# Moving the gather of one channel to steps 12 to 24, loading x first, and sharing weight conversion between engines

## The chip, the cores and the metric

One core of one Trainium2 chip. The metric is device microseconds of one execution of the whole program. A ratio is the mean time of one kernel's fast runs over that of the other's of the same rounds, so it is not quite the ratio of the medians quoted beside it.

## The reference, cut to what matters

```python
# x: (8, 3008, 256) float32; w_in: (256, 2048), w_out: (2048, 256)
X = np.fft.fft(np.fft.fft(x, axis=1), axis=2).real.astype(np.float32)
h = X.reshape(8 * 3008, 256) @ w_in
g = np.where(h > 0, h, np.exp(np.minimum(h, 0)) - 1)     # elu
return (g @ w_out).astype(np.float32)
```

The two weights reach the kernel as 64-bit floats (a float32 array times a NumPy scalar). The kernel converts them to 32 bits itself, with integer and float operations on their words.

## The kernel before

The sequence transform is done with matmuls on folded rows of x (sums and differences of rows s and 3008-s, and of the two halves). The channel transform is folded into w_in ("folding": `fold_block`, four blocks of 512 columns). The main loop has 376 steps. A step takes 256 columns of the transformed data through two of the 16 blocks of d_ff: first matmuls P and Q into a bank H, the elu on VectorE and ScalarE, sums on GpSimd, second matmuls into banks pA to pD. Everything is emitted in an order given by times in `at(t, ...)`, and each engine keeps that order. T is one step.

Channel 128 of the channel transform needs a row of its own: `r128`, spread over all partitions (`Rb`), times the last row of the folded weights, turned into a column (`wex`). Its input is one channel of x for all batches, gathered element by element:

```python
def load_ext(j, s0, s1):                      # 16 calls, 17 DMAs
    def copy(s0, s1, row, step):
        nc.sync.dma_start(out=t[:, s0:s1],
            in_=bass.AP(tensor=xt, offset=x.offset + row * ND + 128,
                        ap=[[SEQ * ND, NB], [step * ND, s1 - s0], [1, 1]]))
    ...
def fold_block(q):                            # w_in's block q times the channel transform
    for part, dst in ((128, Ws), (0, Wc)):
        ps = bank("H")                        # three H banks in all
        for h in range(2):
            mm(ps, CC[:, h*256+part : h*256+part+128], w1[q][:, h], h == 0, h == 1)
        act(dst[:, cols], ps)                 # ScalarE evicts
def spread_last_row(q):
    nc.sync.dma_start(out=wx_dr[:, c], in_=Ws[127:128, c])
    nc.sync.dma_start(out=wex[:, 4*q : 4*q+4], in_=wx_dr[:, c].rearrange(...))
def even_part(i):                             # E of step i waits for wex of its block
    ... scalar_tensor_tensor(out=S.E[:, c], in0=Rb[:, cols(i)],
            scalar=wex[:, f:f+1], in1=S.H[:, c], op0=mult, op1=add)
# schedule
for n in range(16): at((0.5 + 0.55 * n) * T, ... load_ext ...)
at(9.2 * T, get_ext); at(11 * T + 1.35, fold_ext); ...
for q in (1, 2, 3):
    at((2*q - 1) * T + 1.8, fold_block(q)); at((2*q - 1) * T + 1.9, spread_last_row(q))
```

A weight chunk (512 columns of 128 partitions, 16 chunks) is converted by five VectorE operations and one on ScalarE: `fields` (two), `power` (ScalarE), `round` (one), `scale` (two).

Of the kernel before, what the change touches and what calls it, by code (L numbers as in the profile page):

```python
# [75 lines left out]

def _row_consts():

    p = np.arange(128)
    neg = SEQ - 5 - 6 * p  # L80
    last = neg.copy()
    last[0] = SEQ - 6
    return np.stack([neg, HALF - 5 - 6 * p, last], axis=1).astype(np.uint32)


@with_exitstack
def kernel(
# [15 lines left out]
    PK_dr = nc.inline_tensor(_pick_consts(), name="pick_mats")  # L103
    IX_dr = nc.inline_tensor(_row_consts(), name="row_table")

# [23 lines left out]
    xflat = x.rearrange("b s d -> (b s) d")  # L129
    ix = cpool.tile([128, 3], U32, tag="ix")  # L130

    def load_x(b):
        L = [
            spool.tile([128, 6 * ND], FP, tag=f"xl{j}", bufs=1, name=f"xl{j}")
            for j in range(4)
        ]

        for j in (2, 1):
            c = 1 if j == 2 else 2 if b == NB - 1 else 0
            nc.gpsimd.indirect_dma_start(  # L140
                out=L[j],
                out_offset=None,
                in_=xflat,
                in_offset=bass.IndirectOffsetOnAxis(ap=ix[:, c : c + 1], axis=0),
                element_offset=b * SEQ * ND,
            )
        nc.sync.dma_start(out=L[0], in_=xrows(b, 0, 6, 128))
        nc.sync.dma_start(out=L[3], in_=xrows(b, HALF, 6, 128))
        if b == NB - 1:
            nc.gpsimd.dma_start(  # L150
                out=L[1][0:1, 0 : 5 * ND], in_=xrows(b, SEQ - 5, 1, 1, 5)
            )
        return L
# [13 lines left out]
    class Chunk:  # L167



        def __init__(self, src, dst, raw, tmp):
            self.src, self.dst, self.home, self.tmp_tag = src, dst, raw, tmp

        def load(self):
# [21 lines left out]
        def fields(self):  # L196

            if not wide:
                return
            lo, hi, dst = self.parts()  # L200
            if self.tmp_tag == "H":
                t = bank("H").bitcast(I32)
            else:
                t = spool.tile([128, 512], I32, tag=self.tmp_tag, bufs=1, name="pow2")
            self.t = t.rearrange("p (a b) -> p a b", a=dst.shape[1])
            pin(
                nc.vector.tensor_scalar(
                    out=self.t, in0=hi, scalar1=0x7FF00000, scalar2=None,
                    op0=ALU.bitwise_and,
                )  # L210
            )
            pin(
                nc.vector.tensor_scalar(
                    out=dst.bitcast(I32), in0=hi, scalar1=0xFFFFF, scalar2=0x100000,
                    op0=ALU.bitwise_and, op1=ALU.bitwise_or,
                )
            )

        def power(self):

            if not wide:
                return
            act(self.t, self.t, func=AF.Relu, scale=8.0, bias=ebias)

        def round(self):

            if not wide:
                return
            lo, hi, dst = self.parts()
            pin(  # L230
                nc.vector.scalar_tensor_tensor(
                    out=lo.bitcast(FP), in0=lo.bitcast(U32), scalar=2.0**-32,
                    in1=dst.bitcast(I32), op0=ALU.mult, op1=ALU.add,
                )
            )

        def scale(self):

            if not wide:
                return  # L240
            lo, hi, dst = self.parts()
            pin(
                nc.vector.scalar_tensor_tensor(
                    out=self.t, in0=hi, scalar=-(2**31), in1=self.t,
                    op0=ALU.bitwise_and, op1=ALU.bitwise_or,
                )
            )
            pin(
                nc.vector.scalar_tensor_tensor(  # L249
                    out=dst, in0=lo.bitcast(FP), scalar=2.0**-20,  # L250
                    in1=self.t.bitcast(FP), op0=ALU.mult, op1=ALU.mult,
                )
            )

    def w1_dst(c):
        q, half = divmod(c, 2)
        if q not in w1:
# [12 lines left out]
        ("xl3", 1, 6 * ND),  # L270
        ("ot", 2, 1024),
        ("ot", 2, 1024),
        ("ot", 2, 1024),
    ]
    IN_TMP = ("u", "v") + ("H",) * 6
    OUT_TMP = ("H",) * 8
    w1_chunks = [
# [3 lines left out]
            IN_HOMES[c],  # L281
            IN_TMP[c],
        )
        for c in range(8)
# [5 lines left out]
            OUT_HOMES[c],  # L290
            OUT_TMP[c],
        )
        for c in range(8)
# [22 lines left out]
    pick = cpool.tile([128, 32], FP, tag="pick")  # L316
    nc.gpsimd.memset(R4, 0.0)
    nc.gpsimd.memset(Rx4, 0.0)
    zero = cpool.tile([1, 264], BF, tag="zero")
    nc.gpsimd.memset(zero, 0.0)  # L320
    r128_dr = dpool.tile([NB, HALF], FP, tag="r128", name="r128")
# [4 lines left out]
    def bank(tag):  # L326
        bufs = 3 if tag == "H" else 1
        return ppool.tile([128, 512], FP, tag=tag, bufs=bufs, name=tag)

    ACC = ("pA", "pB", "pC", "pD")  # L330

# [112 lines left out]
    def fold_first(L):  # L444
# [5 lines left out]
        vtt(a.unsqueeze(2), c[0], c[1], ALU.add)  # L450
        vtt(g.unsqueeze(2), c[2], c[3], ALU.add)
        e = spool.tile([128, GW], FP, tag="G", bufs=3, name="xb")
        vtt(
# [109 lines left out]
    def fold_ext():  # L563
# [5 lines left out]
        state["xe"] = xe  # L569

    EXT = [(kodd, par) for kodd in range(2) for par in range(2)]

# [15 lines left out]

    def ext_side(g):
        n = NO if g > 1 else NE  # L590
        t = spool.tile([128, NE], FP, tag="bs", bufs=2, name="bs")
        act(t[0:NB, 0:n], state["ext"][32 * g : 32 * g + NB, 0:n])
        state["side", g] = t[0:NB, 0:n]

    def ext_rows(kodd, tt):
        n = NO if kodd else NE
        if not kodd:
            rx = spool.tile([128, HALF + 1], FP, tag="rx", bufs=1, name="rx")
            state["rx"] = rx[0:NB]
            a = state["ext"][0:NB, 0:n]  # L600
        else:
            a = state["side", 2]
# [6 lines left out]
        if not kodd:  # L609
# [4 lines left out]
        nc.sync.dma_start(  # L614
            out=r128_dr[:, base : base + RUN], in_=rx[:, base : base + RUN]
        )
# [305 lines left out]
    exp_neg(warm)  # L922
    nc.sync.dma_start(out=ix, in_=IX_dr.ap())
    w1_chunks[0].load()
    w1_chunks[1].load()
    L_first = load_x(0)
    nc.sync.dma_start(out=CC, in_=CC_dr.ap())
    load_mats(0, 0)
    load_mats(1, 0)
    w1_chunks[2].load()  # L930
    w2_chunks[0].load()
    w1_chunks[3].load()
    w1_chunks[4].load()
    w2_chunks[1].load()
    w1_chunks[5].load()
    EO, ops = fold_x(L_first, lambda key: nc.vector, 1)

# [4 lines left out]
    def dft_now(d, par, tag):  # L942
        d.mms(par, bank(tag))
# [15 lines left out]
    at_chunk(-26.0, w1_chunks[0])  # L959
    at_chunk(-23.0, w1_chunks[1])  # L960
    at(-21.0, lambda: fold_block(0))
    at(-20.9, lambda: spread_last_row(0))
    at(-20.8, w2_chunks[2].load)
    for ri in (0, 1):
        at(-20.7, lambda ri=ri: load_mats(ri, 1))
    at(-20.0, lambda: fold_now("z1 z3 x1 c0 e0 c3 e3 c2 e2 E2 c1 e1 E0 EO0"))
    at(-13.0, lambda: dft_now(R_even, 1, "pA"))
# [8 lines left out]
    at(-12.8, begin_x_even)  # L976
    at(-11.0, lambda: fold_now("o0 o3 o2 O2 o1 O0 EO2"))
    at(-8.5, R_even.copy)
# [113 lines left out]
    for t, fn in (  # L1092
        (-1.8, I_even.copy),
        (0.0, I_even.plus),
        (0.1, I_even.minus),
        (3.1, lambda: dft_now(R_odd, 1, "pB")),
        (3.2, lambda: dft_now(R_odd, 0, "pC")),
        (T + 0.95, R_odd.copy),
        (T + 1.0, R_odd.plus),
        (T + 1.1, R_odd.minus),  # L1100
        (T + 3.1, lambda: dft_now(I_odd, 1, "pD")),
        (T + 3.2, lambda: dft_now(I_odd, 0, "pA")),
        (2 * T + 0.1, I_odd.copy),
        (2 * T + 0.2, I_odd.plus),
        (2 * T + 0.3, I_odd.minus),
    ):
        at(t, fn)
    for n in range(16):
        j, k = divmod(n, 4)
        at(  # L1110
            (0.5 + 0.55 * n) * T,
            lambda j=j, k=k: load_ext(j, 192 * k, 192 * (k + 1)),
        )
    at(9.2 * T, get_ext)
    at(11 * T + 1.35, fold_ext)
    at(11 * T + 4.75, dft_ext)
    at(12 * T + 1.46, lambda: ext_side(1))
    at(12 * T + 1.47, lambda: ext_side(2))
    at(13 * T + 1.0, lambda: ext_rows(0, vtt))
    at(13 * T + 1.46, lambda: ext_side(3))  # L1120
    at(14 * T + 1.35, lambda: ext_rows(1, gtt))
    at(14 * T + 2.0, lambda: spread_ext(0, 1))
    fold_keys = [(k, p) for k in FOLDS for p in range(2 if k[0] not in "czx" else 1)]
# [74 lines left out]
```

## Time and profile before

| | before |
|---|---|
| median of the first 3 runs | 2062.23 us (2056.22 to 2064.47) |
| span of the profiled execution | 2052.9 us |
| TensorE busy / idle in it | 1977.3 / 75.6 us |
| first matmul of steps 0, 3, 8, 17 | 38.53, 99.44, 148.30, 198.08 us |

The profiled execution took 2055.0 us with launch.

From the waits of the first 200 us of the kernel before (who waited for whom: total us, times, longest):

```profile
DVE G L696 <- ACT M L346: 25.0, 3, 9.5
...
DVE e L419 <- ACT xl L346: 6.2, 1, 6.2
```

The first is VectorE, in the steps of the three later foldings, waiting for an exponential (M) on ScalarE; each of the three waits lies between 6 and 9.5 us. The second is the row copy that the prediction speaks of.

### The profile page before, as it was taken

What the parts mean: (1) busy time and instruction counts of PE and PEld (TensorE: products, weight loads), DVE (VectorE), ACT (ScalarE), POOL (GpSimd) and SP (SyncE); (2) the same over time, 40 slices, a digit from 0 to 9 for tenths busy, and PEclk for the clock granted to TensorE, in tenths of its full rate; (3) what the DMA queues carried; (4) which work ended last, traced back from release to release, by engine and by line L of the source; (5) the groups of instructions that cost most, each with busy time, mean ns of one, the idle gap of its engine ahead of it and who ended that gap; (6) DMA issues with size and microseconds to landing.
All of it is one profiled execution on the core that took longest, in us unless ns stands there. A gap on an engine that the chain in (4) does not pass through costs nothing.

```text
span 2052.9 us, 26520 instructions
## 1 busy us (share of the span) xinstructions
PE 1977.3 (96%) x8782; PEld 1646.1 (80%) x8782; DVE 1284.2 (63%) x2356; ACT 851.6 (41%) x1625; POOL 1331.8 (65%) x1833
## 2 busy tenths in 40 slices
PE   6479999999999999999999999999999999999997
PEld 3257888888888888888878888888888888888886
DVE  7466655666566665666566666666656665566665
ACT  1134434444434443444434444444434444344443
POOL 0258865777667775777648776677756776555664
PEclk9799999999999999999999999999999999999999
DMA  8621210021101201012101111102110010100101
GB/s 290 6 93 27 76 26 11 19 51 43 18 11 23 69 19 21 12 31 68 19 11 24 47 42 21 18 19 62 28 23 11 19 18 16 16 11 11 21 11 21
DMA packets 256050, 71.06 MB, mean 35 GB/s; under 512 B 244571, under 2 KB 245353, under 8 KB 255402
## 3 DMA queue, kind: packets, MB, share of 16 engines
q1 hardware_dynamic: 253578, 56.79, 14.3%
q0 software_dynamic: 2336, 12.59, 1.9%
q8 instruction: 69, 1.13, 0.2%
q14 instruction: 67, 0.55, 0.1%
HBM read 44.50 MB, written 24.80 MB: 34 GB/s over the span
## 4 chain that ended last, share of the span: by engine, by line
PE 90%; POOL 1%; DVE 1%; issue 0%; DVEq 0%; ACT 0%; POOLq 0%; ACTq 0%
PE H L334 36%; PE pC L334 16%; PE pB L334 16%; PE pD L334 15%; PE pA L334 7%; POOL G L343 1%; DVE E L670 0%; POOL xl L140 0%; DVE v L340 0%; DVE G L696 0%; POOL e L399 0%; POOL rx L343 0%; DVE Ir L340 0%; DVE u L340 0%; DVE ot L817 0%
## 5 line engine op out<-in xcount | busy, mean ns | idle before, releaser
L343 POOL TENSOR_TENSOR G<-G 128x256 f32<-128x256 f32 x1504 | 1078.9, 728 | 655.3 <-DVE G L696 487.8
L670 DVE SCALAR_TENSOR_TENSOR E<-Rb,wex,H 128x256 f32<-128x256 f32 x752 | 327.9, 477 | 658.2 <-PE H L334 639.5
L346 ACT ACTIVATE G<-H 128x512 f32<-128x512 f32 x376 | 224.5, 597 | 974.4 <-DVE G L680 974.4
L334 PE MATMUL H<-Ir,Ws 128*128 128x256 f32 x1504 | 389.4, 382 | 23.2 <-DVE E L670 23.2
L334 PE MATMUL pC<-G,WT 128*128 128x256 f32 x1504 | 390.3, 382 | 2.3 <-DVE u L340 2.3
L334 PE MATMUL H<-Rr,Wc 128*128 128x256 f32 x1504 | 386.6, 379 | 2.7 <-DVE w L249 1.8
L334 PEld LDWEIGHTS H<-Ir,Ws 128*128 128x128 f32 x1504 | 280.6, 191 | 73.6 <-DVE E L670 25.6
L334 PEld LDWEIGHTS H<-Rr,Wc 128*128 128x128 f32 x1504 | 284.8, 190 | 56.9 <-PE pD L334 1.9
L334 PEld LDWEIGHTS pC<-G,WT 128*128 128x128 f32 x1504 | 282.5, 190 | 54.2 <-issue 13.9
L680 DVE SCALAR_TENSOR_TENSOR G<-E,H 128x512 f32<-128x512 f32 x376 | 255.7, 680 | 26.9 <-POOL G L343 3.5
L696 DVE SCALAR_TENSOR_TENSOR G<-M,G 128x512 f32<-128x512 f32 x376 | 256.3, 682 | 25.0 <-ACT M L346 25.0
L696 DVE SCALAR_TENSOR_TENSOR G<-G,H 128x512 f32<-128x512 f32 x376 | 253.2, 673 | 27.6 <-ACT G L346 27.6
L334 PE MATMUL pB<-G,WT 128*128 128x256 f32 x752 | 229.6, 387 | 4.5 <-POOL G L343 4.4
L346 ACT ACTIVATE G<-G 128x512 f32<-128x512 f32 x376 | 233.3, 620 | 0.0
L334 PE MATMUL pA<-G,w 128*128 128x256 f32 x752 | 223.7, 379 | 1.4 <-DVE Ir L340 1.4
L346 ACT ACTIVATE M<-G 128x512 f32<-128x512 f32 x376 | 224.3, 597 | 0.0
L334 PE MATMUL pD<-G,WT 128*128 128x256 f32 x752 | 224.1, 380 | 0.0
L334 PE MATMUL pD<-G,w 128*128 128x256 f32 x752 | 223.8, 379 | 0.0
L334 PE MATMUL pB<-G,w 128*128 128x256 f32 x752 | 223.7, 379 | 0.0
L346 ACT ACTIVATE M<-M 128x512 f32<-128x512 f32 x376 | 220.9, 588 | 0.1
L334 PEld LDWEIGHTS pB<-G,WT 128*128 128x128 f32 x752 | 138.1, 190 | 39.4 <-POOL G L343 22.9
L334 PEld LDWEIGHTS pA<-G,w 128*128 128x128 f32 x752 | 142.8, 190 | 21.1 <-issue 1.8
(128 smaller groups left out, 1307.5 us busy)
## 6 DMA issues: line engine op xcount, KB each, us to landing
out_dram<-ot SPq DMA_DIRECT2D x504, 32.0 KB
xl<-in_x_dram SPq DMA_DIRECT2D x16, 768.0 KB
MC<-dft_mats SPq DMA_DIRECT2D x4, 1131.0 KB
out_dram<-ot SPq DMA_DIRECT2D x256, 2.0 KB
Rb<-r SPq DMA_DIRECT2D x10, 376.0 KB
raw<-in_moe_w_in_dram SPq DMA_DIRECT2D x6, 512.0 KB
raw<-in_moe_w_out_dram SPq DMA_DIRECT2D x5, 512.0 KB
out_dram<-ot SPq DMA_DIRECT2D x64, 28.0 KB
```

Source lines behind the costliest of these rows:

```text
L334: nc.tensor.matmul(out_, lhsT=lhsT, rhs=rhs, start=start, stop=stop, skip_group_check=True)
L343: pin(nc.gpsimd.tensor_tensor(out=o, in0=a, in1=b, op=op))
L346: pin(nc.scalar.activation(out=o, in_=i, func=func, **kw))
L670: nc.vector.scalar_tensor_tensor(out=S.E[:, c], in0=Rb[:, cols(i)], scalar=wex[:, f : f + 1], in1=S.H[:, c], op0=ALU.mult, op1=ALU.add,)
L680: nc.vector.scalar_tensor_tensor(out=two(S.G[:, 0:512])[:, :, ::-1], in0=two(S.E), scalar=2.0, in1=two(S.H), op0=ALU.mult, op1=ALU.subtract,)
L696: nc.vector.scalar_tensor_tensor(out=o, in0=e, scalar=-1.0, in1=h, op0=ALU.add, op1=ALU.max)
```

## The change

The intent is a shorter head, in four parts: (a) the gather goes to steps 12 to 24, and batch 0's odd half of the special row, which is wanted before that, comes from the x tiles; (b) x is loaded ahead of most weights, the table of row indices is computed by GpSimd instead of loaded, and block 0's folding stands after the first transforms; (c) for 5 of 16 chunks `round` becomes two ScalarE operations and one GpSimd add, and the scratch of four of them moves from the H banks to pA to pD; (d) two folds of batch 0 go to GpSimd, and its odd transforms from steps 0 and 1 to steps 4 to 7. Core of the diff (cuts marked):

```diff
-    nc.sync.dma_start(out=ix, in_=IX_dr.ap())
+    row_tables()                         # four nc.gpsimd.iota
 ...
-    IN_TMP = ("u", "v") + ("H",) * 6
-    OUT_TMP = ("H",) * 8
+    IN_TMP = ("u", "v", "H", "pA", "pC") + ("H",) * 3
+    OUT_TMP = ("pB", "pD") + ("H",) * 6
 ...
         def power(self):
             act(self.t, self.t, func=AF.Relu, scale=8.0, bias=ebias)
+            if self.shared:
+                lo, _, dst = self.parts()
+                act(lo.bitcast(FP), lo.bitcast(U32), scale=2.0**-32)
+                act(dst, dst.bitcast(I32))
         def round(self):
+            if self.shared:
+                gtt(dst, lo.bitcast(FP), dst, ALU.add)
+                return
 ...
+    def dft_ext_0():                     # batch 0's odd row from the x tiles
+        ... mm(ps[g:g+1, 0:NO], state["x_odd"][:, m:m+1], MC[0, 1][:, c:c+NO], ...)
 ...
-    at(-21.0, lambda: fold_block(0))
-    at(-20.9, lambda: spread_last_row(0))
+    at(-12.7, lambda: fold_block(0))     # now after the x_even transforms
+    at(-12.6, lambda: spread_last_row(0))
 ...
-        (3.1, lambda: dft_now(R_odd, 1, "pB")), ... (2 * T + 0.3, I_odd.minus),
+    for step, d in ((4, R_odd), (6, I_odd)):
+        at_half(step, lambda d=d: d, 1, 0)
+        at_half(step + 1, lambda d=d: d, 0, 2 * RUN)
+    at(9 * T + 4.75, dft_ext_0)
+    ... at(11 * T + 2.0, lambda: spread_ext(0, 1))
     for n in range(16):
-        at((0.5 + 0.55 * n) * T, ... load_ext ...)
+        at((12 + 0.75 * n) * T, ... load_ext ...)
-    at(9.2 * T, get_ext)
-    at(11 * T + 1.35, fold_ext)
+    at(24.4 * T, get_ext)
+    at(25 * T + 1.35, fold_ext)
     ... (the rest of that row likewise 14 steps later)
```

More of the change, by code (lines that the diff above doesn't have):

```diff
@@ L74, in _pick_consts @@
     return m
-def _row_consts():
-    p = np.arange(128)
-    neg = SEQ - 5 - 6 * p
-    last = neg.copy()
-    last[0] = SEQ - 6
-    return np.stack([neg, HALF - 5 - 6 * p, last], axis=1).astype(np.uint32)
 @with_exitstack
@@ L103 @@
     PK_dr = nc.inline_tensor(_pick_consts(), name="pick_mats")
-    IX_dr = nc.inline_tensor(_row_consts(), name="row_table")
     cpool = ctx.enter_context(tc.tile_pool(name="consts", bufs=1))
@@ L129, with row_tables @@
     xflat = x.rearrange("b s d -> (b s) d")
-    ix = cpool.tile([128, 3], U32, tag="ix")
+    ix = cpool.tile([128, 3], I32, tag="ix")
+    def row_tables():
+        for c, n, base in (
+            (1, 128, HALF - 5),
+            (0, 128, SEQ - 5),
+            (2, 128, SEQ - 5),
+            (2, 1, SEQ - 6),
+        ):
+            pin(
+                nc.gpsimd.iota(
+                    ix[0:n, c : c + 1], pattern=[[0, 1]], base=base, channel_multiplier=-6
+                )
+            )
     def load_x(b):
@@ L143, in load_x @@
                 in_=xflat,
-                in_offset=bass.IndirectOffsetOnAxis(ap=ix[:, c : c + 1], axis=0),
+                in_offset=bass.IndirectOffsetOnAxis(
+                    ap=ix[:, c : c + 1].bitcast(U32), axis=0
+                ),
                 element_offset=b * SEQ * ND,
             )
+        nc.sync.dma_start(out=L[3], in_=xrows(b, HALF, 6, 128))
         nc.sync.dma_start(out=L[0], in_=xrows(b, 0, 6, 128))
-        nc.sync.dma_start(out=L[3], in_=xrows(b, HALF, 6, 128))
         if b == NB - 1:
@@ L167, with __init__ @@
     class Chunk:
-        def __init__(self, src, dst, raw, tmp):
+        def __init__(self, src, dst, raw, tmp, shared=False):
             self.src, self.dst, self.home, self.tmp_tag = src, dst, raw, tmp
+            self.shared = shared
         def load(self):
@@ L200, in fields @@
             lo, hi, dst = self.parts()
-            if self.tmp_tag == "H":
-                t = bank("H").bitcast(I32)
+            if self.tmp_tag in ("H",) + ACC:
+                t = bank(self.tmp_tag).bitcast(I32)
             else:
@@ L229, in round @@
             lo, hi, dst = self.parts()
+            if self.shared:
+                gtt(dst, lo.bitcast(FP), dst, ALU.add)
+                return
             pin(
                 nc.vector.scalar_tensor_tensor(
-                    out=lo.bitcast(FP), in0=lo.bitcast(U32), scalar=2.0**-32,
+                    out=dst, in0=lo.bitcast(U32), scalar=2.0**-32,
                     in1=dst.bitcast(I32), op0=ALU.mult, op1=ALU.add,
@@ L249, in scale @@
                 nc.vector.scalar_tensor_tensor(
-                    out=dst, in0=lo.bitcast(FP), scalar=2.0**-20,
+                    out=dst, in0=dst, scalar=2.0**-20,
                     in1=self.t.bitcast(FP), op0=ALU.mult, op1=ALU.mult,
@@ L270 @@
         ("xl3", 1, 6 * ND),
-        ("ot", 2, 1024),
+        ("rx", 1, HALF + 1),
         ("ot", 2, 1024),
@@ L274 @@
     ]
-    IN_TMP = ("u", "v") + ("H",) * 6
-    OUT_TMP = ("H",) * 8
+    ACC = ("pA", "pB", "pC", "pD")
+    IN_TMP = ("u", "v", "H", "pA", "pC") + ("H",) * 3
+    OUT_TMP = ("pB", "pD") + ("H",) * 6
     w1_chunks = [
@@ L282 @@
             IN_TMP[c],
+            c in (2, 3, 4),
         )
@@ L291 @@
             OUT_TMP[c],
+            c < 2,
         )
@@ L316 @@
     pick = cpool.tile([128, 32], FP, tag="pick")
-    nc.gpsimd.memset(R4, 0.0)
-    nc.gpsimd.memset(Rx4, 0.0)
+    nc.vector.memset(R4, 0.0)
+    nc.vector.memset(Rx4, 0.0)
     zero = cpool.tile([1, 264], BF, tag="zero")
-    nc.gpsimd.memset(zero, 0.0)
+    nc.vector.memset(zero, 0.0)
+    row_tables()
     r128_dr = dpool.tile([NB, HALF], FP, tag="r128", name="r128")
@@ L328, in bank @@
         return ppool.tile([128, 512], FP, tag=tag, bufs=bufs, name=tag)
-    ACC = ("pA", "pB", "pC", "pD")
     def mm(out_, lhsT, rhs, start, stop=True):
@@ L451, in fold_first @@
         vtt(g.unsqueeze(2), c[2], c[3], ALU.add)
+        d = state["x_odd"] = spool.tile([128, 6], FP, tag="xd", bufs=1, name="xd")
+        vtt(d, a, g, ALU.subtract)
         e = spool.tile([128, GW], FP, tag="G", bufs=3, name="xb")
@@ L569, in fold_ext @@
         state["xe"] = xe
+    def dft_ext_0():
+        ps = state["ext"] = bank("H")
+        for t in range(3):
+            for par in range(2):
+                m, c = 2 * t + par, par * BW + t * NE
+                g = 32 * (2 + par)
+                mm(
+                    ps[g : g + 1, 0:NO],
+                    state["x_odd"][:, m : m + 1],
+                    MC[0, 1][:, c : c + NO],
+                    t == 0,
+                    t == 2,
+                )
     EXT = [(kodd, par) for kodd in range(2) for par in range(2)]
@@ L587, in dft_ext, with ext_side, ext_rows @@
                 )
-    def ext_side(g):
+    def ext_side(g, rows=NB):
         n = NO if g > 1 else NE
         t = spool.tile([128, NE], FP, tag="bs", bufs=2, name="bs")
-        act(t[0:NB, 0:n], state["ext"][32 * g : 32 * g + NB, 0:n])
-        state["side", g] = t[0:NB, 0:n]
-    def ext_rows(kodd, tt):
+        act(t[0:rows, 0:n], state["ext"][32 * g : 32 * g + rows, 0:n])
+        state["side", g] = t[0:rows, 0:n]
+    def ext_rows(kodd, tt, rows=NB):
         n = NO if kodd else NE
+        if not kodd or rows < NB:
+            rx = spool.tile([128, HALF + 1], FP, tag="rx", bufs=1, name="rx")
+            state["rx"] = rx[0:rows]
         if not kodd:
-            rx = spool.tile([128, HALF + 1], FP, tag="rx", bufs=1, name="rx")
-            state["rx"] = rx[0:NB]
             a = state["ext"][0:NB, 0:n]
@@ L614, in ext_rows @@
         nc.sync.dma_start(
-            out=r128_dr[:, base : base + RUN], in_=rx[:, base : base + RUN]
+            out=r128_dr[0:rows, base : base + RUN], in_=rx[:, base : base + RUN]
         )
@@ L922 @@
     exp_neg(warm)
-    nc.sync.dma_start(out=ix, in_=IX_dr.ap())
     w1_chunks[0].load()
+    L_first = load_x(0)
     w1_chunks[1].load()
-    L_first = load_x(0)
+    load_mats(0, 0)
     nc.sync.dma_start(out=CC, in_=CC_dr.ap())
-    load_mats(0, 0)
-    load_mats(1, 0)
-    w1_chunks[2].load()
-    w2_chunks[0].load()
-    w1_chunks[3].load()
-    w1_chunks[4].load()
-    w2_chunks[1].load()
-    w1_chunks[5].load()
-    EO, ops = fold_x(L_first, lambda key: nc.vector, 1)
+    EO, ops = fold_x(
+        L_first, lambda key: nc.gpsimd if key in ("EO1", "EO3") else nc.vector, 1
+    )
     def fold_now(keys):
@@ L959, with load_rest @@
     at_chunk(-26.0, w1_chunks[0])
-    at_chunk(-23.0, w1_chunks[1])
-    at(-21.0, lambda: fold_block(0))
-    at(-20.9, lambda: spread_last_row(0))
+    def load_rest():
+        ops["x1", 0]()
+        act(MC[1, 0][0:1, 0:1], L_first[1][0:1, 0:1])
+        load_mats(1, 0)
+        for chunk in (
+            w1_chunks[2], w1_chunks[3], w2_chunks[0], w1_chunks[4], w2_chunks[1],
+            w1_chunks[5], w2_chunks[5],
+        ):
+            chunk.load()
+    at(-25.5, load_rest)
+    at(-25.0, lambda: fold_now("z1 z3 c3 e3 c2 e2 E2 o3 o2"))
+    at_chunk(-24.0, w1_chunks[1])
+    at(-22.0, lambda: fold_now("c0 e0 c1 e1 E0 EO0"))
     at(-20.8, w2_chunks[2].load)
@@ L965 @@
         at(-20.7, lambda ri=ri: load_mats(ri, 1))
-    at(-20.0, lambda: fold_now("z1 z3 x1 c0 e0 c3 e3 c2 e2 E2 c1 e1 E0 EO0"))
     at(-13.0, lambda: dft_now(R_even, 1, "pA"))
@@ L976 @@
     at(-12.8, begin_x_even)
-    at(-11.0, lambda: fold_now("o0 o3 o2 O2 o1 O0 EO2"))
+    at(-12.7, lambda: fold_block(0))
+    at(-12.6, lambda: spread_last_row(0))
+    at(-11.0, lambda: fold_now("O2 o0 o1 O0 EO2"))
     at(-8.5, R_even.copy)
@@ L1095 @@
         (0.1, I_even.minus),
-        (3.1, lambda: dft_now(R_odd, 1, "pB")),
-        (3.2, lambda: dft_now(R_odd, 0, "pC")),
-        (T + 0.95, R_odd.copy),
-        (T + 1.0, R_odd.plus),
-        (T + 1.1, R_odd.minus),
-        (T + 3.1, lambda: dft_now(I_odd, 1, "pD")),
-        (T + 3.2, lambda: dft_now(I_odd, 0, "pA")),
-        (2 * T + 0.1, I_odd.copy),
-        (2 * T + 0.2, I_odd.plus),
-        (2 * T + 0.3, I_odd.minus),
     ):
         at(t, fn)
+    for step, d in ((4, R_odd), (6, I_odd)):
+        at_half(step, lambda d=d: d, 1, 0)
+        at_half(step + 1, lambda d=d: d, 0, 2 * RUN)
+    at(9 * T + 4.75, dft_ext_0)
+    for g in (2, 3):
+        at(10 * T + 1.46, lambda g=g: ext_side(g, 1))
+    at(11 * T + 1.35, lambda: ext_rows(1, gtt, 1))
+    at(11 * T + 2.0, lambda: spread_ext(0, 1))
     for n in range(16):
@@ L1110 @@
         at(
-            (0.5 + 0.55 * n) * T,
+            (12 + 0.75 * n) * T,
             lambda j=j, k=k: load_ext(j, 192 * k, 192 * (k + 1)),
         )
-    at(9.2 * T, get_ext)
-    at(11 * T + 1.35, fold_ext)
-    at(11 * T + 4.75, dft_ext)
-    at(12 * T + 1.46, lambda: ext_side(1))
-    at(12 * T + 1.47, lambda: ext_side(2))
-    at(13 * T + 1.0, lambda: ext_rows(0, vtt))
-    at(13 * T + 1.46, lambda: ext_side(3))
-    at(14 * T + 1.35, lambda: ext_rows(1, gtt))
-    at(14 * T + 2.0, lambda: spread_ext(0, 1))
+    at(24.4 * T, get_ext)
+    at(25 * T + 1.35, fold_ext)
+    at(25 * T + 4.75, dft_ext)
+    at(26 * T + 1.46, lambda: ext_side(1))
+    at(26 * T + 1.47, lambda: ext_side(2))
+    at(27 * T + 1.0, lambda: ext_rows(0, vtt))
+    at(27 * T + 1.46, lambda: ext_side(3))
+    at(28 * T + 1.35, lambda: ext_rows(1, gtt))
     fold_keys = [(k, p) for k in FOLDS for p in range(2 if k[0] not in "czx" else 1)]
```

## The prediction

> **What bounds the kernel now.** I read the page's busy table first, then the 40 slices, then the windows of the first 160 us, then the waits of the first 200 us, and last the timeline where the longest wait lies.
>
> ```profile
> PE 1977.3 (96%) x8782; PEld 1646.1 (80%) x8782; DVE 1284.2 (63%) x2356; ACT 851.6 (41%) x1625; POOL 1331.8 (65%) x1833
> ...
> PE   6479999999999999999999999999999999999997
> PEclk9799999999999999999999999999999999999999
> DMA  8621210021101201012101111102110010100101
> ```
>
> TensorE is busy 96% of 2052.9 us, so only 75.6 us of its idle time can be won, and the slices show nearly all of it in the first three (51.3 us each). From slice four on TensorE is full and sets the pace: two neighbouring steps in the timeline start at 172.40 and 177.26, 4.86 us, and a step is 22 matmul records at about 0.2165 us = 4.76 us. A change that removes no matmuls can only win in the head. There the windows say:
>
> ```profile
> 40.00:50.00 10.00, 5.88 (x11) 3.74 (x12) 9.83 (x19) 2.31 (x4) 0.86 (x2) 0.67 0.77 154
> 50.00:60.00 10.00, 4.32 (x12) 2.44 (x12) 6.16 (x11) 2.37 (x5) 2.22 (x4) 0.84 0.90 2
> 60.00:70.00 10.00, 9.31 (x18) 4.19 (x17) 2.01 (x4) 2.28 (x4) 1.20 (x2) 0.64 0.93 5
> 70.00:80.00 10.00, 4.16 (x16) 2.57 (x14) 3.59 (x6) 2.10 (x4) 3.19 (x6) 1.00 0.80 7
> 80.00:90.00 10.00, 0.00 (x0) 0.00 (x0) 0.00 (x0) 0.00 (x0) 0.00 (x0) 0.55 0.67 14
> ```
>
> The columns are the stretch, its length, busy time (and count) of PE, PEld, DVE, ACT and POOL, granted clock, DMA share and GB/s. From 50 to 90 us the DMA engines are 67 to 93% busy and move 2 to 14 GB/s, and from 80 to 90 no engine computes. The waits and the timelines name it:
>
> ```profile
> DVE E L670 <- DMA wex<-wx: 18.7, 2, 18.4
> ...
> 39.51 18.56 SPq L536 DMA_DIRECT2D x<-in_x_dram  x8
> 60.62 10.46 SPq L536 DMA_DIRECT2D x<-in_x_dram  x5
> 88.34 0.38 SPq L365 DMA_DIRECT2D wx<-Ws  x1
> 90.04 0.38 SPq L367 DMA_DIRECT2D wex<-wx  x1
> ...
> 92.28 0.87 DVE L670 SCALAR_TENSOR_TENSOR E<-Rb,wex,H 128x256 f32<-128x256 f32 x2 [18.40 <-DMA wex<-wx]
> ```
>
> The gather of channel 128 (17 loads of single elements) holds the SyncE queue from 39.5 to 88 us. The 2 KB copy wx<-Ws stands behind it: its source was ready when ScalarE ended at 62.97, it was issued at 88.34, and step 2 waited 18.4 us for the column wex that comes out of it. The rest of the head's loss is a chain over VectorE (13 weight chunks converted in steps 0 to 7) and over the weight folding on TensorE:
>
> ```profile
> 58.59 3.75 PE L334 MATMUL H<-w,CC 128*128 128x512 f32 x4 [5.68 <-DVE G L696]
> 63.02 3.78 PE L334 MATMUL H<-w,CC 128*128 128x512 f32 x4 [0.69 <-ACT Ws L346]
> 130.23 1.96 PE L334 MATMUL H<-w,CC 128*128 128x512 f32 x4 [2.88 <-DVE G L696]
> ```
>
> The same four matmuls take 3.75 us at 58 us and 1.96 us at 130 us: half speed after idling.
>
> **What the Trainium skill says.** "DMA: Bandwidth & Descriptors", the best-practice table: a strided, non-contiguous last dimension "Lowers to one descriptor per element". The trace agrees: 7 GB/s at a DMA share of 0.80. The same page, "Queues, rings and completion order": on each DMA engine one issuer's descriptors are consumed in ring order; so a small copy behind the gather is late even once issued. Here the delay seen is already at issue. "TensorE: Matmul & The Clock Gate", Part 1: after about 3.4 us of idling the array runs at half rate until it has been busy as long. The pair 3.75 and 1.96 us agrees. "GPSIMD Engine Reference", Engine selection: two-input elementwise work is about twice as slow on GpSimd as on VectorE. Here 128x384 takes 1.00 us on GpSimd and 128x768 takes 0.95 us on VectorE, so it agrees.
>
> **The change part by part.** (a) *Gather moved to steps 12 to 24.* It removes the 18.4 us wait, and the cold restart after it (the matmuls at 93 to 97 us run at half rate, about 2.5 us). SyncE's order in the changed program has wx and wex of block 1 right after the weight loads, so no wait takes its place. In its new place the gather is 17 loads that took some 40 to 46 us of DMA here (39.5 to 88, less some 7 us in which 3 MB of weights passed too); twelve steps are 58 us, so it fits. The tile stores that share the time need about 8 us a tile at most, and the second tile's stand behind the gather in the issue order; their buffer is wanted again only at step 35. The gathered rows are wanted at step 25. I count no cost. Block 0's odd row, wanted at step 16, now comes from the x tiles: 6 more matmuls (two column groups at once; the present 12 in four groups took 2.02 us from 170.38 to 172.40, so again about 1.9 us on TensorE), one tiny VectorE add, two GpSimd operations of 0.98 us. Cost +2 us.
>
> (b) *x first, no index table.* VectorE starts the first fold at 10.66 and ends EO0 at 25.3, with 6.2 us waiting for a ScalarE copy of one row that stood behind the first folding (which waited 9.5 us for CC). Now the row copy comes before it. My chain: first conversion 5.0 to 6.4, x rows at 8 to 11 us, five fold operations at 0.9, rest of the conversion 1.35, chunk 1 3.1, four more folds 3.6: EO0 at 21 to 22. But the first folding (8 records of 0.43 = 3.5 us), which ran at 15.8 to 21.3 in idle time, now stands between the transforms: 21.2 + 5.8 (two cold transforms) + 3.8 + 3.5 + 3.8 = 38.1, against 38.53 now. Step 0 starts where it did; gain 0 to 2 us.
>
> (c) *Conversion.* For 5 of 16 chunks one VectorE operation (0.69 us) becomes two on ScalarE (0.60 each) and one on GpSimd (128x512, about 1.45 us from 0.728 for 128x256). VectorE saves 3.5 us, EO1 and EO3 save 1.9 more. But the chain of a chunk grows: power, two copies and the add are 0.66 + 1.2 + 1.45 = 3.3 us before the last VectorE operation, against some 1.7 us of other VectorE work meanwhile, so I expect short VectorE stalls of 1 to 2 us in steps 0 and 1. Their scratch lies in banks pA to pD instead of the three H banks, and the odd transforms (4 x 1.9 us) leave steps 0 and 1 for steps 4 to 7. That frees an H bank for the first half of block 1's folding, now waiting 5.7 us; the second half still waits for the elu of step 0.
>
> Sum, by the start of E in a step: step 0 at 41 to 42 (now 43.2). Step 1: VectorE work 6 us + stalls 2, E at 49.5 to 50.5. Step 2: folding, evictions and elu of step 0 end at 59, then 4 us of VectorE: 63 to 65 (now 92.28), 28 us ahead. Steps 3 to 5 with VectorE at 8.5 us a step and one folding wait of 7 us: step 6 near 107 (now about 138), 30 us ahead. Then the odd transforms, which fall where TensorE is nearly full, give back 3 to 4 us, and part (a) 2 us. Net 24 to 26 us. The three runs of before lie at 2056 to 2064, the profiled one at 2055; from about 2059, less 25, I predict **2034 us**.
>
> **Rivals.** *VectorE is the real bound of the head:* then the 18.4 us come back as VectorE work queued behind. Against it: VectorE is 100% idle in that wait, and its conversions proceed in order with the steps, so nothing was done ahead. It would leave 8 to 12 us of gain: 2048. *The whole backlog dissolves:* freed banks and a warm array leave VectorE's bare work (about 59 us from E of step 0 to E of step 8, at 43.2 + 59 = 102 against some 149 now) as the only bound: 40 to 45 us of gain, 2016. Against it: the elu's bank and the two evictions of each folding stay in order. *The gather costs in its new place:* stores, row spreads or GpSimd waiting for the gathered rows at step 25. For it: single elements took 80% of DMA time. Against it: two steps of slack. It would give back up to 10 us: 2044. *The index iota is slow to start on GpSimd* and delays two of the four x loads, by perhaps 3 to 6 us: 2038; no row of this trace shows an iota.
>
> **Range and chances.** The gain is 18 to 42 us for nearly all these; below that only with two rivals at once. 2016 to 2050 should hold it 8 in 10. Over 2% faster is below 2021: 0.14, the second rival or part of it. Slower by 2% needs a loss of 41 us where TensorE is full: 0.01. Within 2%: 0.85.
>
> **What would show it.** Right: no wait for wex over 2 us; step 0's first matmul near 38 us; E of step 2 at 62 to 66; the first matmul of step 8 near 120 (now 148.30); TensorE's busy time up by about 2 us at full clock and its idle time down by some 25; single-element loads between 170 and 240 us with TensorE full there. Wrong: a stall of GpSimd on xs or of VectorE on ot near steps 24 to 28; step 0 starting after 42 (iota, x late); VectorE waiting over 10 us in steps 0 to 5 for GpSimd's adds; or a head under 105 us at step 8.

## The result, and the profile after

The changed kernel takes 2040.53 us (median of 4 runs, 2038.72 to 2043.5) beside 2063.35 us of the kernel before (4 runs, 2056.22 to 2066.01). The ratio is 0.9896, 95% interval 0.9867 to 0.9925: 1.0% faster, some 21.5 us, inside the predicted range and 6.5 us above the predicted time.

The 40 slices of the changed kernel:

```profile
PE   5699999999999999999999999999999999999997
...
PEclk9899999999999999999999999999999999999999
DMA  8107410121001210111101111002110110100101
```

Slice three, 7 tenths before, is 9 now, and slice two is 6 instead of 4. The element loads show as the 7 and 4 in slices four and five (153 to 255 us), where TensorE stays at 9. The same stretches as in the prediction, with the same columns:

```profile
40.00:50.00 10.00, 5.40 (x16) 3.77 (x16) 7.17 (x15) 4.33 (x8) 6.26 (x4) 0.76 0.48 163
50.00:60.00 10.00, 3.59 (x7) 1.76 (x7) 6.28 (x12) 6.07 (x12) 4.47 (x6) 0.67 0.00 0
60.00:70.00 10.00, 7.55 (x19) 4.33 (x18) 5.38 (x10) 4.18 (x8) 6.37 (x9) 0.72 0.04 2
70.00:80.00 10.00, 6.63 (x22) 5.09 (x22) 9.41 (x17) 3.47 (x6) 5.14 (x8) 0.83 0.00 0
80.00:90.00 10.00, 6.38 (x14) 2.91 (x14) 2.85 (x5) 1.98 (x4) 0.73 (x1) 0.83 0.23 79
```

No stretch is empty now, and the DMA engines rest from 50 to 80 us. But only VectorE, from 70 to 80 us, is over 90% busy, and TensorE's granted clock stays at 0.67 to 0.83: a chain of short waits has taken the place of the long one. SyncE's timeline shows the small copies issued as soon as their source is there, and the gather much later:

```profile
60.80 0.25 SPq L381 DMA_DIRECT2D wx<-Ws  x1
61.98 0.38 SPq L383 DMA_DIRECT2D wex<-wx  x1
...
168.51 11.72 SPq L554 DMA_DIRECT2D x<-in_x_dram  x7
...
182.78 10.57 SPq L554 DMA_DIRECT2D x<-in_x_dram  x5
```

The waits of the head that are left, from the waits of the first 300 us of the changed kernel:

```profile
POOL G L359 <- DVE G L730: 62.8, 25, 7.5
...
PE pA L350 <- DVE e L415: 16.1, 1, 16.1
...
DVE G L730 <- ACT M L362: 20.0, 3, 7.5
...
PE H L350 <- DVE G L730: 11.4, 3, 6.4
...
DVE Rr L356 <- ACT bs L362: 9.5, 1, 9.5
...
DVE w L263 <- POOL w L359: 5.6, 4, 1.8
```

There is no line for wex any more. VectorE waits 20.0 us for the exponential M (25.0 before), 9.5 us for the copy bs of the first transform, which is new, and 5.6 us in four waits for the GpSimd adds, which is new too. Where each step begins (the first of its P matmuls in TensorE's timeline, us):

| step | 0 | 1 | 2 | 3 | 6 | 8 | 17 |
|---|---|---|---|---|---|---|---|
| before | 38.53 | 51.88 | 71.60 | 99.44 | 137.28 | 148.30 | 198.08 |
| changed | 41.42 | 48.91 | 64.83 | 76.22 | 116.80 | 131.56 | 178.24 |
| lead | -2.9 | 3.0 | 6.8 | 23.2 | 20.5 | 16.7 | 19.8 |

Most of the lead, 16.4 of 23.2 us, is made between the starts of steps 2 and 3, in the place of the wait for wex. Step 0 starts later than before. Some of the lead is lost again to the odd transforms in steps 4 to 7, as the prediction said, and some comes back in steps 11 to 16, where the kernel before computed its special row (7.02, 5.52 and 5.82 us for steps 11, 14 and 15, against 4.92, 4.74 and 4.75 now). That is not all kept: the changed kernel computes its row in step 25, which takes 6.86 us, and at the start of step 26 the lead is 17.7 us. Over the whole of the two profiles it is 16.0 us (2052.9 less 2036.9).

### The profile page after: what moved, and what is told of

The parts are those of the page before. It is cut to its first block, busy times and chain, and to the rows that moved or that the text cites. A ratio compares the mean times of both kernels' runs of the same rounds, so it can differ in the third digit from the quotient of the medians.

```text
span 2036.9 us, 26573 instructions
## 1 busy us (share of the span) xinstructions
PE 1974.3 (97%) x8794; PEld 1645.6 (81%) x8794; DVE 1278.7 (63%) x2353; ACT 858.1 (42%) x1638; POOL 1343.5 (66%) x1843
## 2 busy tenths in 40 slices
DMA packets 256181, 71.59 MB, mean 35 GB/s; under 512 B 244444, under 2 KB 245226, under 8 KB 255532
## 4 chain that ended last, share of the span: by engine, by line
PE 93%; DVE 3%; POOL 2%; issue 1%; DMA 1%; ACT 0%; SPq 0%; DVEq 0%; POOLq 0%; ACTq 0%
PE H L350 38%; PE pC L350 16%; PE pB L350 16%; PE pD L350 15%; PE pA L350 8%; POOL G L359 1%; DMA xl<-in_x_dram,ix 0%; DVE G L730 0%; DVE E L704 0%; DVE w L263 0%; DVE e L415 0%; DVE H L214 0%; DMA raw<-in_moe_w_out_dram 0%; DVE H L257 0%; DVE w L245 0%
## 5 line engine op out<-in xcount | busy, mean ns | idle before, releaser
L350 PEld LDWEIGHTS pC<-G,WT 128*128 128x128 f32 x1504 | 282.0, 190 | 53.8 <-issue 13.9
L350 PEld LDWEIGHTS pB<-G,WT 128*128 128x128 f32 x752 | 138.3, 190 | 36.5 <-POOL G L359 19.8
```

The lines of the kernel that those rows point to most:

```text
L350: nc.tensor.matmul(out_, lhsT=lhsT, rhs=rhs, start=start, stop=stop, skip_group_check=True)
```

## The experiments

Theory A: the moved gather is nearly the whole gain, and the rest of the change nets about zero. Rival B: loading, folding order and conversion bring a third or more. Rival C: the gather costs something in its new place. The first four ran on one chip, beside 11 runs of the kernel before (median 2060.02 us).

**The gather alone.** The kernel before, with only part (a):

```diff
 (kernel before)
+    vtt(d, a, g, ALU.subtract)                 # x_odd
+    at(9 * T + 4.75, dft_ext_0) ... at(11 * T + 2.0, spread_ext(0, 1))
-        at((0.5 + 0.55 * n) * T, ... load_ext ...)
+        at((12 + 0.75 * n) * T, ... load_ext ...)
-    at(9.2 * T, get_ext) ...
+    at(24.4 * T, get_ext) ...
```

> The kernel before with one thing changed: the gather at steps 12 to 24 and batch 0's odd row from the x tiles; loads, folding and conversion as before. Theory A (the moved gather is nearly the whole gain, the rest of the change nets about zero): 16 to 22 us faster than before, ratio 0.989 to 0.992, step 0 still near 38.5 us, no wait for wex above 2 us, step 8 near 130. Rival B (the rest of the change brings a third or more of the gain): only 6 to 14 us faster, ratio 0.993 to 0.997, step 8 at 136 or later.

Measured: 2041.39 us (median of 6), ratio 0.9896 (0.9874 to 0.9919), the same ratio as the whole change. Step 0 at 38.77, step 8 at 128.42, step 17 at 177.57 us. Theory A holds, B is out: the other parts together add nothing to the time that these runs can resolve (the intervals are some 5 us to either side).

**The gather back.** The changed kernel with part (a) undone (the home of one raw chunk and its load go back too, since they shared the gather's tile):

```diff
-        at((12 + 0.75 * n) * T, ... load_ext ...)
+        at((0.5 + 0.55 * n) * T, ... load_ext ...)
-    at(24.4 * T, get_ext) ...
+    at(9.2 * T, get_ext) ...
```

> The changed kernel with only the gather undone: it stands in steps 0.5 to 9 again, no odd row from the x tiles. Theory A: the whole gain is lost, ratio to before 0.995 to 1.003, a wait for wex of 15 us or more in step 2. Rival B: at most two thirds of the gain lost, ratio 0.992 to 0.995.

Measured: 2059.99 us, ratio 0.9993 (0.997 to 1.0016). The wait is back, longer than before. From its waits of the first 170 us:

```profile
DVE E L704 <- DMA wex<-wx: 23.4, 1, 23.4
```

In this kernel steps 0 to 2 start early as in the changed one (63.21 us for step 2), but step 3 starts at 98.38, as before at 99.44. What the other parts win ahead of the gather is waited away at its end: the gather's end sets that point, not the work before it.

**No shared conversion.** The changed kernel, part (c) half undone:

```diff
-            c in (2, 3, 4),
+            False,
-            c < 2,
+            False,
```

> The changed kernel with the shared conversion undone: all 16 chunks convert on VectorE, the scratch banks stay. Theory A: the four stalls of VectorE for GpSimd's add (5.6 us together) go and 3.5 us of VectorE work come back, so within 3 us of the changed kernel either way (ratio to before 0.988 to 0.991). Rival B: sharing is part of the gain, so this is 4 us or more slower than the changed kernel (ratio 0.992 or more).

Measured: 2036.65 us, ratio 0.9874 (0.9852 to 0.9896), outside what I expected, on the fast side. The next run, which leaves sharing as it is, took 2041.56 us in the same rounds. Sharing seems to cost time; a pair further down settles that.

**No gather at all.** The changed kernel with the 17 loads replaced by zeros (wrong, relative error 0.056):

```diff
-        copy(...)                              # all element loads
+        if j == 0 and s0 == 0:
+            pin(nc.gpsimd.memset(state["x1"][0 : 4 * NB, 0:768], 0.0))
```

> The changed kernel with the 17 element loads replaced by zeros written once by GpSimd (wrong in channel 128 and its neighbours, on purpose). Theory A: the gather costs nothing in its new place, so within 2 us of the changed kernel (ratio to before 0.988 to 0.990). Rival C (it slows stores, row spreads or GpSimd in steps 12 to 28): 4 us or more faster than the changed kernel, ratio 0.987 or less, with steps 12 to 27 shorter.

Measured: 2041.56 us, ratio 0.9898 (0.9875 to 0.9921): not faster. Steps 13 to 17 take 4.74 to 4.75 us each with the loads and without. As a mean cost of 4 us or more, rival C is out.

But the profiles show where it could come from. GpSimd folds the gathered rows (xs) in step 25. In the changed kernel's profile it did so at 218.45 us, and the last read of the rows had been issued at 212.52, so it did not wait. In the profiled execution of the run with the gather alone the same loads were slower. From its timeline of SyncE:

```profile
182.79 14.04 SPq L538 DMA_DIRECT2D x<-in_x_dram  x5
```

and from its waits between 170 and 260 us:

```profile
POOL xs L343 <- DMA xs<-xe_dr: 6.7, 1, 6.7
...
PE H L334 <- POOL xe L343: 5.7, 1, 5.7
```

Five loads took 14.04 us to issue instead of 10.57, the rows came late, and TensorE stood for 5.7 us. That happened in three profiled executions (GpSimd waited 6.7, 1.9 and 3.2 us: the gather alone, no sharing, the foldings after the exponential), and each was its kernel's slowest run, by 4.1, 4.7 and 3.4 us over the next. TensorE itself waited 5.7, 0.9 and 2.2 us for the rows in them, so the late rows can't be all of the difference, in the second least of all. The place has little room; what a late gather costs a run was not measured alone.

The next four ran on another chip, beside 11 runs of before (median 2055.69 us). They ask why the other parts net zero, and whether more is to be had.

**Block 0's folding later.** In the changed kernel VectorE waited 9.5 us for bs, the ScalarE copy of the first transform. ScalarE's order has the two evictions of block 0's folding ahead of it.

```diff
-    at(-12.7, lambda: fold_block(0))
-    at(-12.6, lambda: spread_last_row(0))
+    at(-8.45, lambda: fold_block(0))           # after R_even.copy at -8.5
+    at(-8.44, lambda: spread_last_row(0))
```

> The changed kernel with block 0's folding and its two evictions put after the ScalarE copy of the first transform (no data changes). In the changed kernel VectorE waited 9.5 us for that copy, which stood behind both evictions, and TensorE began step 0 at 41.4 us instead of my 38.1. Theory D (that order is what made step 0 late, and step 0 sets the rest): step 0 at 38 to 39.5 us and 1.5 to 3 us faster than the changed kernel (ratio to before near 0.988 to 0.989). Rival: later waits (folding of block 1) take it up, step 0 earlier but step 3 where it was, no change in the time.

Measured: 2038.18 us, ratio 0.9902 (0.9872 to 0.9931). Step 0 starts at 38.76 us instead of 41.42. From TensorE's timeline, of the changed kernel and then of this run (first transform, third transform, and the transform after the folding):

```profile
22.29 4.14 PE L350 MATMUL pA<-MC,e 128*128 128x377 f32 x6 [16.05 <-DVE e L415]
...
29.04 2.07 PE L350 MATMUL pC<-MC,xb 128*128 128x377 f32 x6
...
37.51 2.17 PE L350 MATMUL pA<-MC,o 128*128 128x377 f32 x6 [1.06 <-ACT bs L362]
```

```profile
22.34 3.63 PE L350 MATMUL pA<-MC,e 128*128 128x377 f32 x6 [16.08 <-DVE e L415]
...
27.72 2.06 PE L350 MATMUL pC<-MC,xb 128*128 128x377 f32 x6
...
34.95 2.06 PE L350 MATMUL pA<-MC,o 128*128 128x377 f32 x6
```

The wait for bs is gone, and with the slower restart after it that is 1.3 of the 2.7 us. The other 1.4 us lie in the first two transforms, which took 6.75 us there and 5.38 here although the edit comes after them; in five other profiled executions with the old order they took 5.35 to 6.76 us. So the order is shown as about half of the delay; the other half varies from one execution to the next. Step 3 starts at 73.90 (76.22) and step 6 at 118.00 (116.80), but a second profile of the unaltered changed kernel (further down) has 75.85 and 119.94. So whether later waits take up the gain, as the rival says, is not settled, and the time does not resolve it.

**Foldings 1 to 3 after the exponential.**

```diff
-        at((2 * q - 1) * T + 1.8, lambda q=q: fold_block(q))
-        at((2 * q - 1) * T + 1.9, lambda q=q: spread_last_row(q))
+        at((2 * q - 1) * T + 2.25, lambda q=q: fold_block(q))
+        at((2 * q - 1) * T + 2.26, lambda q=q: spread_last_row(q))
```

> The changed kernel with the foldings of blocks 1 to 3 emitted just after the next exponential and after mm_Q, instead of before them. In the changed kernel the last exponential of steps 0, 2 and 4 stands on ScalarE behind the two evictions of a folding, and VectorE waited for it 5.05 us in step 1, 7.49 us in step 3 and once more in step 5 (20.0 us in all, most of what idles in steps 0 to 5). Theory E (that order is the largest loss left in the head): these waits fall below 2 us each and the kernel is 6 to 12 us faster than the changed one, ratio to before 0.983 to 0.987. Rival F: TensorE then waits for the folding's eviction at the next step, under 3 us of gain.

Measured: 2031.7 us, ratio 0.9871 (0.9841 to 0.99), 6.5 us under the run before it in the same rounds (which differs in block 0's folding too). From its waits of the first 170 us:

```profile
DVE E L704 <- DMA wex<-wx: 8.0, 1, 8.0
...
DVE G L730 <- ACT M L362: 1.4, 1, 1.4
```

The 20 us for M are gone but for 1.4, as theory E says (its range of ratios ended at 0.987). Part of it turned into a new wait: wex is made later and arrives late once, 8.0 us. Step 6 starts at 110.13, step 17 at 171.59 us.

**All scratch in the H banks.** The changed kernel without sharing, and with the old banks:

```diff
-    IN_TMP = ("u", "v", "H", "pA", "pC") + ("H",) * 3
-    OUT_TMP = ("pB", "pD") + ("H",) * 6
+    IN_TMP = ("u", "v") + ("H",) * 6
+    OUT_TMP = ("H",) * 8
```

> The changed kernel without the shared conversion and with all conversion scratch in the three H banks again, as before the change. Against the run without sharing alone it tells what the scratch banks bring. My prediction said that they free an H bank for block 1's folding: 2 to 6 us slower than without sharing (ratio to before 0.989 to 0.991). Rival: the folding waits for the elu of the step before in either case, so within 1.5 us.

Measured: 2039.93 us, ratio 0.9913 (0.9884 to 0.9943). Its partner ran on the other chip at 0.9874, and the two intervals overlap. It points to a gain of the banks of several us, but these runs do not settle it. The two traces agree with the prediction's mechanism: here the first half of block 1's folding waits 4.76 us for VectorE's elu, and in the run without sharing alone it starts without a wait; from the start of step 0 to that of step 3 it is 35.6 us here and 31.8 there.

**Both foldings moved, no sharing.** The edits of the two folding runs and of the run without sharing together:

> The changed kernel with block 0's folding after the copy, blocks 1 to 3's folding after the exponential, and all conversion on VectorE again. If the three gains add: 2 + 9 + 4 us faster than the changed kernel, 2024 to 2030 us, ratio 0.982 to 0.985. If VectorE's own work is the next bound, removing sharing costs some 3 us here: 0.985 to 0.987.

Measured: 2026.98 us (2025.68 to 2028.2), ratio 0.9847 (0.9818 to 0.9876), as expected if the gains add; the interval reaches into the other range too, so the pair below has to settle it.

The last four ran together, beside 11 runs of before (median 2060.55 us), so that they can be compared directly. First the changed kernel, unaltered:

> The changed kernel unaltered, for comparison on this chip: ratio to before 0.987 to 0.992. In its first profile the gathered rows landed some 6 us before GpSimd wanted them; in profiled executions of three variants the loads were slower and GpSimd waited 1.9 to 6.7 us. Either may be seen here.

Measured: 2041.44 us (2040.93 to 2042.2), ratio 0.9905 (0.9881 to 0.9928). Its gathered rows were in time. Its profile shows how far two profiles of one kernel differ: step 3 starts at 75.85 us (76.22 in the first profile), step 6 at 119.94 (116.80). The foldings of step 3 in TensorE's timeline, first profile and then this one:

```profile
83.06 3.45 PE L350 MATMUL H<-w,CC 128*128 128x512 f32 x4 [2.93 <-DVE G L730]
87.20 1.98 PE L350 MATMUL H<-w,CC 128*128 128x512 f32 x4 [0.69 <-ACT Ws L362]
```

```profile
82.69 3.75 PE L350 MATMUL H<-w,CC 128*128 128x512 f32 x4 [2.20 <-DVE G L730]
87.13 3.78 PE L350 MATMUL H<-w,CC 128*128 128x512 f32 x4 [0.69 <-ACT Ws L362]
```

Here the second half too ran at half clock (3.78 instead of 1.98 us), and so it did in step 5. So 3 us at step 6 between two single profiles are no effect of an edit. Then both foldings moved, sharing kept:

> The changed kernel with both foldings moved (block 0 after the copy, blocks 1 to 3 after the exponential), the shared conversion kept. Against the same without sharing it tells what sharing costs when the folding waits are gone. If sharing costs through the stalls for GpSimd's adds as it did before (some 4 us): 3 to 6 us slower than without sharing. Rival: with fewer folding waits VectorE's own work binds, and sharing then helps by 2 us or more.

Measured: 2031.09 us (2029.2 to 2032.46), ratio 0.9856 (0.9832 to 0.9879): moving the foldings alone is worth 10.4 us against the changed kernel beside it. Then the same without sharing:

> Both foldings moved, all conversion on VectorE, again beside the changed kernel on one chip: 10 to 14 us faster than the changed kernel, ratio to before 0.982 to 0.986.

Measured: 2027.09 us (2026.49 to 2028.21), ratio 0.9837 (0.9814 to 0.9861): 14.4 us faster than the changed kernel (10 to 14 expected), and no run of one overlaps the other. Between the last two kernels, all six runs apart, lie 4.0 us: that is what sharing costs. The stalls of VectorE for the adds are the same with the foldings moved as without. From the waits of the first 170 us of the run with both foldings moved and sharing kept:

```profile
DVE E L704 <- DMA wex<-wx: 6.4, 1, 6.4
...
DVE w L263 <- POOL w L359: 5.6, 4, 1.8
```

In the profiles of these two runs step 0 starts at the same time (39.16 and 39.17 us), step 1 starts 1.2 us later with sharing, step 3 2.9 and step 6 3.3: the loss arises in steps 0 to 2, where the shared chunks stand. The stalls of 5.6 us less the 3.5 us of saved VectorE work are 2.1 of the 4.0 us. The profile with sharing also has a wait of 1.4 us for M, which the other has not; the rest was not traced.

Last, the use of the gathered rows six steps later (the row's own work and its spread with it):

```diff
-    at(24.4 * T, get_ext)
-    at(25 * T + 1.35, fold_ext) ...
+    at(30.4 * T, get_ext)
+    at(31 * T + 1.35, fold_ext) ...
```

> As the run before in this list, with the use of the gathered rows six steps later (fold at step 31 instead of 25), which leaves about 29 us more room for a slow gather; still in time for step 47. If slow gathers cost time in some executions only: the same fastest run within 1 us, no run more than 3 us above it, no wait of GpSimd for xs. Rival: the rows are always in time, then nothing changes at all.

Measured: 2026.71 us (2025.39 to 2028.85), ratio 0.9836 (0.9812 to 0.9859). Nothing changes: GpSimd did not wait for xs in the profile of this run or of the one before it. GpSimd folds the rows at 236.90 us, some 37 us after the last read was issued at 199.46. It is the safer place; that it saves time was not shown.

## Why the prediction was right, and where it was off

**What bounds the head.** Right. The first rival (VectorE work queued behind the wait) predicted 8 to 12 us of gain; the gather alone gives the whole ratio of 0.9896, and taking it back gives 0.9993. One sentence of the range does not fit the rivals: a gain under 18 us was said to need two of them at once, but this one alone was put at 8 to 12.

**Part (a).** Right in its main term: the wait of 18.4 us is gone and nothing replaced it, and step 3 starts 23.2 us earlier. The extra transform was priced at 1.9 us and took 2.06 (at 141.35 us). The gather ran from 168.51 to the last issue at 212.52 us, 44 us, priced at 40 to 46. "I count no cost" holds for the mean; "two steps of slack" does not: the last read was issued 5.9 us before its use, and a late one took about 2.4 us from issue to landing in the run with the gather alone (222.14 to 224.51 us), which leaves an estimated 3.5 us, less than one step. In three profiled executions the rows were 1.9 to 6.7 us too late, which is the stall of GpSimd on xs that the prediction named as a sign of being wrong.

**Part (b).** The step that failed. "21.2 + 5.8 + 3.8 + 3.5 + 3.8 = 38.1" has only TensorE's terms, and step 0 began at 41.42. EO0 did end at 22.2 us, and the folding ran where I put it. Three terms of about 1 us each make the difference: the first transform started at 22.29 instead of 21.2, the two cold ones took 6.75 us instead of 5.8, and TensorE waited 1.06 us for bs, which has no term. For ScalarE's order was not in the sum: the copy bs stood behind both evictions, ended at 37.5 instead of near 27, and held back VectorE for 9.5 us and TensorE's next transform. VectorE then still had its rows and the first shared chunk to do, so E of step 0 came at 46.13 us instead of 41 to 42. Moving the folding put step 0 at 38.76 and E at 43.82 us; it shows the order as one cause, worth 1.3 us at step 0, and not as the only one.

**Part (c).** "Short VectorE stalls of 1 to 2 us in steps 0 and 1" was too small a term: 1.78, 0.65, 1.67 and 1.48 us, 5.6 together, against 3.5 us of VectorE work saved. I had both sides of this and did not draw the sum, 2.1 us lost. Sharing costs 4.0 us where it could be measured alone; these stalls are about half of that. The first half of block 1's folding did start without a wait, and the second half waited for the elu of step 0, 6.4 us, as I wrote. In the foldings of steps 3 and 5 the waits were 7.5 us each, near the 7 us I took, but their first halves ran at half clock too (3.45 and 3.50 us, where 1.98 is the full-speed time), which I had not counted.

**The sum.** Together these put E of step 2 at 69.1 us (I wrote 63 to 65) and step 6 at 116.8 (near 107), so the lead was 20.5 us there and not 30. I expected 5 to 6 us of it to be given back and 25 us to stay; in the two profiles 16.0 stayed, in the runs 21.5. Of the signs named for "right", two came: no wait for wex, and the loads where TensorE is full. Step 0 (41.42, not near 38), E of step 2 (69.1, not 62 to 66) and step 8 (131.56, not near 120) missed. So did the busy-time check: TensorE's busy time fell by 3.0 us instead of rising by 2 (it rose by 1.3 in the second profile of the changed kernel, so the sign is open), and its idle time by 13.0 (13.9), not 25. Block 0's folding had left idle time, so TensorE waits 16.1 us in one piece before its first transform; and the profile of before was of a fast execution. So the number came closer than its working. The steps were read from a profile of 2055.0 us, the 25 us were taken off 2059, and the runs of before had a median of 2063.35: that the total is only 6.5 us off is in part luck, while its main term, the wait, is shown.

**The second rival** (the whole backlog dissolves, 2016 us) stayed out for the reason given: the exponential and the two evictions keep ScalarE's order. Moving the foldings behind the exponential took that away and won 10.4 us together with moving block 0's folding. The rival that the iota delays the x loads is out: the first indirect load was issued at 1.78 us, against 2.71 before.

**Open.** Why identical kernels differ by up to 16 us between runs (before: 2052.07 to 2068.38 on one chip) is not settled; late rows explain at most some us, and only where the gather ends close to its use. The record shows one thing that goes with it: in each of the three lists of 11 runs the quickest run of before had a mean granted clock of 0.987 or 0.988 and the slowest 0.981 to 0.983. Which of the two causes the other is not shown. What the scratch banks bring alone is open as well, and loading x first, the computed index table and the later odd transforms were never run alone.

## What to carry to other kernels

Here a bulk of tiny transfers hurt most through what stood behind it in the same queue (18.4 us for a copy of 2 KB): look for the smallest copy that a compute engine waits for, and move the bulk to where nothing urgent follows. When work is taken off a full engine and given to two idle ones, add up the new chain: here the engine that waits for the answer lost more (5.6 us) than it saved (3.5 us). And a folding, eviction or copy put "into the gap" of one engine also takes a place in another engine's order: check what stands behind it there.

## What the Trainium skill lacked or had wrong

- "DMA: Bandwidth & Descriptors", Rules for kernel authors: it says that single-element access lowers to one descriptor per element, which fits: with the 24,576 elements not loaded, the trace holds 24,712 fewer packets under 512 B (219,732 against 244,444). It gives no rate or spread for them. Here five loads of 1536 elements (7680 elements of 4 bytes) took 10.57 us to issue in one execution and 14.04 in another.
- The same page, Queues, rings and completion order, describes ring order inside a DMA engine. The harm came earlier, at issue: a ready 2 KB copy was issued 25 us after its source, because SyncE was still at the element loads.
- "GPSIMD Engine Reference", Engine selection, names GpSimd as the engine for iota but gives no time: four of 128x1 or less took 0.47 us together. Its rule that two-input work is about twice as slow there agrees: the 128x512 add took 1.29 us, a two-input VectorE operation of that size 0.69.
- "TensorE: Matmul & The Clock Gate", Part 1, gives an idle window of about 3.4 us as what brings the half rate. Four folding matmuls took 3.75 us after 6.4 us of idling, which agrees, and 1.98 us where TensorE had idled only 0.69 us (87.20 us). But in step 5 of the changed kernel they took 3.50 us after only 2.01 us of idling (106.30 us), with the granted clock at 1.00 from 105 to 106 us and at 0.50 from 107 to 108; in the kernel before they took 1.96 us after 2.88. So here the bare length of the last idle time did not decide it.
